# Four edits to a layernorm, windowed-attention and gated-FFN kernel: load order of the inputs, duplicated columns on GpSimd, a third early tile, and another rule for placing the value products

## The chip, the cores and the metric

The kernel runs on one core of a Trainium2 chip. A core has five engines that run their own instruction lists side by side and meet through semaphores: TensorE (PE in the profile; PEld are its weight loads), VectorE (DVE), ScalarE (ACT), GpSimd (POOL) and SyncE (SP, which here only issues DMAs). The metric is the device time of one execution in microseconds. Before the change three runs gave 557.07 (median), 558.04 and 556.71.

## The reference

The input x is 2048 rows of 576 bf16 values. It is normalised by row, and two branches read the result; x plus their product is the output.

```
xn = layernorm(x)                                   # eps 1e-5, no scale, no shift
qkv = xn @ wqkv                                     # 576 -> 3 x 32 heads x 18
s  = softmax(mask(q k^T / sqrt(18))) v @ wo         # key within the last 256 rows, not after the query
g  = silu((sigmoid(xn @ w_gate) * (xn @ w_up)) @ w_down)    # 576 -> 4608 -> 576
out = x + s * g
```

## The kernel before

**Chunks.** The rows go in four chunks of 512 (c = 0 to 3), each of four blocks of 128. For each chunk there are: normalising and transposing x; the value projection ("v"); five groups of query and key projections ("qk"); scores, exponentials and masks for eight groups of four heads ("sc", "ex", "mk"), each group in five score bins; two *value-product runs* ("pv"), each for four head groups, 256 TensorE instructions in chunk 0 (8 key blocks) and 384 in the others (12); the output projection ("wo"); 36 gate-and-up tiles of 128 hidden columns ("f1", each in two halves, "f10" and "f11"); and the down projection ("f2"). Weights for gate and up are read from HBM again in each chunk, two tiles at a time (`weights`), w_down only once.

**Pairs.** Every product has a contraction of 576 = 64 + 4 x 128 rows. TensorE is used as two halves of 64 rows: `pair` (the matmul of line 124) sends a matmul to each half, and the two run together. For the odd 64 rows both halves need the same data, so x is kept with its first 64 columns twice: `xnr` has 640 columns, 0 to 63 a duplicate ("dup") of 64 to 127. The remainder weights (`wgr`) are the matching 64 rows.

**The opening (chunk 0).** `load_x` issues the four x blocks first, all with `X_PRIO` 0. For each block, `build_ln` computes statistics (VectorE, lines 537 to 543, then a power on POOL, line 545; block 2 instead in two passes on ScalarE with small steps on POOL, lines 596 to 600), normalises on VectorE (`norm`, line 553), copies the duplicate on VectorE (`f_dup`, line 557), transposes on TensorE (line 609) and evicts to `xnT` (line 586; ScalarE, the last block on VectorE). Meanwhile `warm` keeps TensorE busy with 43 pairs on zeros and 10 more behind the first transposes. `NEARLY` = 2 tiles are "early": cut into four parts of 128 rows, so each part can start when its block of xnT is there. Around the last part `ahead` puts the first half of the next tile.

**The order of the work.** Nothing here loops on the chip. `build_graph` makes all operations with their dependencies, a duration and a priority (10 ns for each step of it), and `schedule` places them in Python: among those ready on an engine it takes the one with the smallest start time plus priority, at planned times. Each engine's instruction list is then fixed, and on the chip each operation waits on semaphores for what it needs. So the planner's estimates set the order, not the durations. A DMA's planned landing is its issue, 2.5 us and its bytes, plus a `slack` of its own; the moves of attention outputs (`oT<-o2T`) have 1.0 us.

**PSUM.** It has four units of two banks. Pool S (units 0, 1) serves transposes, projections and scores, pool F (2, 3, 1) the tiles and the down projection, pool V (any two) the value products.

**Placing value-product runs.** TensorE's instructions are counted in `at`. `fits` looks at the marks 193 + 256 k of that count: a run may start only where at most `FETCH_MAX` = 248 of its instructions lie in the 320 before any mark. If it doesn't fit, other operations go first until it does.

## Time and profile before

| | |
|---|---|
| time, median of 3 (lowest, highest) | 557.07 us (556.71, 558.04) |
| the profiled execution | 556.95 us, span 555.7 us |
| TensorE busy | 550.3 us, 99% of the span |
| VectorE, ScalarE, GpSimd busy | 58%, 49%, 38% of the span |
| DMA | 75.87 MB, mean 137 GB/s; 228 to 272 GB/s in the first seven fortieths of the span |
| first transposes, first tile | 5.70 us, 7.50 us |
| last matmul group | ends at 553.21 us |

A line of the chain gives start, duration, and the engine, tile and line that held the chain there; "issue" is time in which nothing that the profile shows was waited for. A line of the timeline gives start, duration, engine, line, operation, output tile <- inputs, shape, count, and in brackets how long the engine was idle before and what ended that. A line of the stretches gives the stretch, its length, TensorE's busy time in it (matmuls that start in it), the granted clock as a share, the share of DMA time in use, and GB/s. Matmul ends are modelled, so waits are best read from their starts. Times in the texts that have no line beside them are from the trace's single records: starts of matmuls, packets of a DMA queue, and landings.

### The profile page before, as it was taken

To read this page: it belongs to the slowest core of one execution; us is meant where nothing else is said; L and a number is where in the kernel's file an instruction comes from. 1 tells how busy PE (TensorE), PEld (TensorE's weight loads), DVE (VectorE), ACT (ScalarE), POOL (GpSimd) and SP (SyncE) were. 2 spreads that over 40 slices of the span, in tenths; PEclk is the share of its full clock that TensorE was granted. 3 is DMA by queue.
4 is the path that set the end of the run, shared out by engine and by line. 5 is a ranking of instruction groups with operands and counts; after the bars stand their busy time and mean duration, and the time that the engine had idled before them with its cause. 6 is when DMAs were issued, how large, how long until landed. Compare 5 with 4: busy or idle time off the path is not lost.

```text
span 555.7 us, 19419 instructions
## 1 busy us (share of the span) xinstructions
PE 550.3 (99%) x8342; PEld 339.3 (61%) x8342; DVE 323.4 (58%) x782; ACT 272.4 (49%) x379; POOL 208.7 (38%) x360
## 2 busy tenths in 40 slices
PE   8999999999999999999999999999999999999998
PEld 7454445777555654467775554447788644454787
DVE  5467567745858667537645567557535865474011
ACT  4246564442646647553455646654555477423201
POOL 5634343845424336434531517540922280011000
DMA  8999999442267654671243646554132255532010
GB/s 228 252 272 239 258 241 246 126 95 40 53 169 232 176 160 133 189 129 34 51 134 106 197 125 184 155 151 106 41 97 61 75 156 151 164 86 77 2 45 24
DMA packets 141213, 75.87 MB, mean 137 GB/s; under 512 B 43676, under 2 KB 139260, under 8 KB 141128
## 3 DMA queue, kind: packets, MB, share of 16 engines
q1 hardware_dynamic: 133704, 68.71, 46.9%
q0 software_dynamic: 7424, 5.92, 4.1%
q8 instruction: 66, 1.08, 0.8%
q14 instruction: 19, 0.16, 0.1%
HBM read 63.18 MB, written 2.36 MB: 118 GB/s over the span
## 4 chain that ended last, share of the span: by engine, by line
PE 96%; DMA 1%; POOL 1%; DVE 1%; issue 0%; ACT 0%
PE ps L124 93%; PE ps L813 3%; DMA oT<-o2T 1%; DMA x<-in_A_x_dram 0%; POOL kx L727 0%; POOL qk L286 0%; POOL oT L286 0%; DVE small L537 0%; DVE small L539 0%; DVE xnr L553 0%; PE ps L609 0%; DVE xnr L557 0%; DVE small L541 0%; ACT thf L1083 0%; DVE small L543 0%
## 5 line engine op out<-in xcount | busy, mean ns | idle before, releaser
L124 PE MATMUL ps<-xnT,wgs 64*128 64x512 bf16 (+1 forms) x2400 | 283.8, 368 | 0.1
L763 ACT ACTIVATE expr<-ps 128x1024 bf16<-128x1024 f32 (+4 forms) x160 | 154.9, 968 | 79.2 <-PE ps L124 77.5
L124 PEld LDWEIGHTS ps<-xnT,wgs 64*128 64x128 bf16 x2400 | 113.3, 94 | 111.9 <-issue 0.8
L124 PE MATMUL ps<-wd_sb,hT 64*128 64x288 bf16 (+2 forms) x2448 | 154.0, 276 | 0.0
L970 ACT ACTIVATE tring<-ps 128x512 bf16<-128x512 f32 x144 | 86.1, 598 | 125.4 <-PE ps L124 122.6
L973 DVE SCALAR_TENSOR_TENSOR hT<-tring,ps 128x512 bf16<-128x512 bf16 x144 | 98.6, 685 | 78.1 <-ACT tring L970 75.5
L286 POOL DMA_DIRECT2D qk<-qd x160 | 82.8, 524 | 150.8 <-PE ps L124 145.4
L124 PEld LDWEIGHTS ps<-wd_sb,hT 64*128 64x128 bf16 x2448 | 113.1, 94 | 28.0
L776 DVE TENSOR_TENSOR expr<-expr,mask 128x128 bf16<-128x128 bf16 (+2 forms) x240 | 64.5, 295 | 68.7 <-ACT expr L763 67.7
L286 POOL DMA_DIRECT2D oT<-o2T x72 | 36.9, 519 | 106.2 <-DVE o2T L849 51.4
L727 POOL TENSOR_SCALAR kx<-kprev,small 128x256 bf16<-128x256 bf16 x64 | 60.5, 955 | 7.8 <-PE ps L124 6.8
L124 PE MATMUL ps<-qk,kx 64*128 64x320 bf16 (+1 forms) x704 | 59.2, 254 | 0.0
L124 PE MATMUL ps<-xnT,wgr 64*128 64x512 bf16 (+1 forms) x300 | 55.9, 367 | 0.0
L124 PEld LDWEIGHTS ps<-qk,kx 64*128 64x128 bf16 x704 | 31.8, 94 | 25.8 <-ACT expr L763 1.3
L124 PE MATMUL ps<-xnT,wqg 64*128 64x512 bf16 (+1 forms) x320 | 37.7, 355 | 0.0
L648 DVE CAST qd<-ps 128x1024 bf16<-128x1024 f32 (+1 forms) x20 | 22.3, 1116 | 7.2 <-PE ps L124 7.2
L727 DVE TENSOR_SCALAR kx<-qk,small 128x512 bf16<-128x512 bf16 x64 | 22.2, 370 | 6.1 <-PE ps L124 5.8
L124 PEld LDWEIGHTS ps<-xnT,wgr 64*128 64x128 bf16 x300 | 14.8, 94 | 16.6
L841 DVE STREAM_TRANSPOSE ot<-ps 128x512 f32<-128x512 f32 x32 | 20.1, 685 | 7.4 <-PE ps L813 7.4
L849 DVE STREAM_TRANSPOSE o2T<-o 128x512 bf16<-128x512 bf16 x32 | 22.7, 708 | 0.5
L124 PEld LDWEIGHTS ps<-xnT,wqg 64*128 64x128 bf16 x320 | 15.2, 94 | 12.0 <-issue 0.3
L1085 DVE TENSOR_TENSOR thf<-thf,s_attn 128x576 bf16<-128x576 bf16 (+2 forms) x5 | 2.0, 399 | 34.2 <-ACT thf L1083 34.2
(68 smaller groups left out, 294.7 us busy)
## 6 DMA issues: line engine op xcount, KB each, us to landing
wgs<-in_B_w_gate_dram SPq DMA_DIRECT2D x72, 256.0 KB, 3.5
wgs<-in_B_w_up_dram SPq DMA_DIRECT2D x72, 256.0 KB, 4.0
wd_sb<-in_B_w_down_dram SPq DMA_DIRECT2D x9, 576.0 KB, 5.8
wqg<-in_A_wqkv_dram SPq DMA_DIRECT2D x32, 128.0 KB, 3.2
qk<-qd POOLq DMA_DIRECT2D x100, 36.0 KB, 2.5
wgr<-in_B_w_gate_dram SPq DMA_DIRECT2D x36, 64.0 KB, 2.6
wgr<-in_B_w_up_dram SPq DMA_DIRECT2D x36, 64.0 KB, 3.0
wvo<-in_A_wqkv_dram SPq DMA_DIRECT2D x4, 576.0 KB, 4.9
```

The source lines that it names most:

```text
L124: res = eng.matmul(outs[i], lhs(ROWS[t], i), rhs(ROWS[t], i), start=start, stop=stop, tile_position=(64 * t, 0))
L286: o = self.op(eng, DMA_ISSUE_NS[eng], lambda e: e.dma_start(dst, src), name, deps, prio, nbytes=nbytes)
L648: return eng.tensor_copy(dst, self.both(h, n))
L727: return e.tensor_scalar(self.kx[:, sx, pos:pos + n_ // SW, t, :], src.rearrange("p (s k) -> p s k", k=SW), self.half[:, t:t + 1], None, A ...
L763: return eng.activation(self.expr[:, se, :, lo * SW:NT], self.both(h, NT)[:, :, lo * SW:NT], ACTF.Exp, scale=SM_SCALE)
L776: return eng.tensor_tensor(e_, e_, m_, ALU.mult)
L813: res = eng.matmul(outs[i][p0:p0 + VH, cols], self.v_aug[ROWS[i], o:o + VH], self.expr[ROWS[i], se, t, cols], start=m == 0, stop=m == len( ...
L841: return e.transpose(self.ot1[:, p1, :], self.halves(hp, NT, un)[i])
L849: t2 = op("DVE", dve_ns(NT), lambda e, p2=p2, p3=p3: e.transpose(self.o2T[:, p3, :], self.o2[:, p2, :]), f"ot2:{c}:{pr}:{i}", deps=[on, d3 ...
L970: th = op("ACT", act_ns(NT), lambda e: e.activation(self.tring[:, st, :], bank(h, 0), ACTF.Tanh, scale=0.5), f"th:{c}:{ft}", deps=[pg, dt_ ...
L973: mu = op("DVE", dve_ns(NT), lambda e: e.scalar_tensor_tensor(self.hT[:, ft, :], self.tring[:, st, :], 1.0, bank(h, 1), ALU.add, ALU.mult) ...
L1085: q2 = op("DVE", dve_ns(w, 2.0), lambda e: e.tensor_tensor(t, t, s_, ALU.mult), f"fq2:{nm}", deps=[th, self.op_s[sb]], prio=0)
```

## The change

What the planner's tables and rules change to:

- The fourth x block gets priority 1.8 and is thereby issued behind the first gate and up weights and the two remainders. In the opening, landings of x and of the first four weight loads are planned by one running total of bytes (256 bytes per ns) with a fixed latency each, and no longer by single slacks.
- In chunk 0 the duplicate is computed on POOL, from x and the statistics (`norm_rem`), and no longer copied from the normalised block; transposes wait for both.
- Three tiles are early. The third is cut in two parts: rows of blocks 0 to 2, and of block 3. The first half of the tile behind them takes PSUM unit 0 (pool_a). One warm-up pair less.
- `fits` asks for time: the instructions of each 320 before a mark must last at least 6.1 us by plan, or 4.25 us while less than 256 tile instructions of the chunk are left. Each instruction of a run counts 6.3 ns, one behind it 54 or 30.6 ns, those before it as planned.
- Moves of attention outputs are planned with 1.8 us of slack (before 1.0); the spacing of scores, some durations on VectorE and POOL, the release of PSUM units (100 ns for pools S and V, before 60) and the size of the remainder loads are planned with other numbers.

The core of the diff; what is left out are unused names and the plumbing of new fields:

```diff
-FETCH_MAX = 248
+FETCH_NS = (6100.0, 4250.0)
+RUN_NS = 6.3
+STEP_NS = (54.0, 30.6)
...
-X_PRIO = (0, 0, 0, 0)
+X_PRIO = (0, 0, 0, 1.8)
...
-DUP_ACT = ()
+DUP_POOL = (0, 1, 2, 3)
...
-NWARM = (43, 10)
-NEARLY = 2
-FIRST_SLACK_NS = (-800.0, -1500.0)
+NWARM = (42, 10)
+NEARLY = 3
+OPEN_NS = 2000.0
+OPEN_BYTES_PER_NS = 256.0
+X_LAT_NS = (300.0, 800.0, 800.0, 800.0)
+W_LAT_NS = 1000.0
...
-PARTS = (((0, 1), (1, 2), (2, 3), (3, 4)),) * NEARLY
+PARTS = (((0, 1), (1, 2), (2, 3), (3, 4)),) * 2 + (((0, 3), (3, 4)),)
...
-SPACE_NS = (2000, 2000, 2000, 1700)
+SPACE_NS = (1900, 1700, 2200, 1800)
...
+        self.late = PE_IN_NS if name == "F" else POOL_IN_NS
...
-                free.append((max(now, max(r.end for r in h.rel) + PE_IN_NS), self.units.index(u), u))
+                free.append((max(now, max(r.end for r in h.rel) + self.late), self.units.index(u), u))
...
         self.pool_f = Pool("F", [2, 3, 1], last)
+        self.pool_a = Pool("F", [0], last)
...
-        return [self.dma(dst[ROWS[1 - t], :], src[0:RD, :], RD * src.shape[1] * 3, name, lane + (t,), deps=deps, prio=prio)
+        return [self.dma(dst[ROWS[1 - t], :], src[0:RD, :], RD * src.shape[1] * 2, name, lane + (t,), deps=deps, prio=prio)
...
+            def norm_rem(e, mean=mean, rstd=rstd, x_in=x_in, sn=sn, op0=ALU.add if on_act else ALU.subtract):
+                return e.tensor_scalar(self.xnr[:, sn, 0:RD], x_in[:, 0:RD], mean, rstd, op0, ALU.mult)
...
-            dup_act = c == 0 and i in DUP_ACT
-            dup = op("ACT" if dup_act else "DVE", act_ns(RD) if dup_act else 180, f_dup, f"ln:dup:{st}", deps=[ap], prio=pr)
-            self.ln_dup = dup
+            if c == 0 and i in DUP_POOL:
+                dup = op("POOL", 300, norm_rem, f"ln:dup:{st}", deps=[rs, ag, dn], prio=pr)
+            else:
+                dup = op("DVE", 180, f_dup, f"ln:dup:{st}", deps=[ap], prio=pr)
+            self.ln_dup = [ap, dup]
...
-                o.slack = 1000.0
+                o.slack = 1800.0
...
-                   prio=3 if part is None else 1, odeps=chain[half] if part is None else list(behind), acq=acq,
+                   prio=3 if part is None else 1 + ft / 2, odeps=chain[half] if part is None else list(behind), acq=acq,
...
-                        ahead = self.pool_f.hold()
+                        ahead = self.pool_a.hold()
...
-    @staticmethod
-    def fits(at, n):
-        ahead = (FETCH_AT - at) % FETCH
-        parts = [ahead] if n >= ahead else []
-        edge = ahead
-        while edge < n:
-            parts.append(min(n, edge + FETCH) - max(0, edge - FETCH_AHEAD))
+    def fits(self, at, n, st, places, ffn):
+        def when(p):
+            if p < at:
+                return next(t0 + (p - a0) * w for a0, t0, w in reversed(places) if a0 <= p)
+            return st + TURN_NS + min(p - at, n) * RUN_NS + max(p - at - n, 0) * STEP_NS[ffn]
+        edge = at + (FETCH_AT - at) % FETCH
+        while edge - FETCH - FETCH_AHEAD < at + n:
+            if edge > at and when(edge) - when(edge - FETCH - FETCH_AHEAD) < FETCH_NS[ffn]:
+                return False
             edge += FETCH
-        return max(parts, default=0) <= FETCH_MAX
+        return True
...
-                    if o.run and not self.fits(at + len(self.new_waits(o, known)) // 2, o.run):
+                    st = max(free[e], ready_t[o.cidx])
+                    if o.run and not self.fits(at + len(self.new_waits(o, known)) // 2, o.run, st, places, int(ffn[phase] < FETCH)):
...
+                if o.lat is not None:
+                    moved = max(moved, stt + o.est + 700.0) + o.nbytes / OPEN_BYTES_PER_NS
+                    o.end = moved + o.lat
```

## The prediction

> **What bounds the kernel now.** I read the page first (who is busy), then stretches of the span (where TensorE is not), then the chain and TensorE's timeline in those places. The profiled execution took 556.95 us for a span of 555.70, so 1.25 us lie outside the span; it stands 0.12 us under the median of 557.07.
>
> ```profile
> PE 550.3 (99%) x8342; PEld 339.3 (61%) x8342; DVE 323.4 (58%) x782; ACT 272.4 (49%) x379; POOL 208.7 (38%) x360
> ...
> q8 instruction: 66, 1.08, 0.8%
> ...
> PE 96%; DMA 1%; POOL 1%; DVE 1%; issue 0%; ACT 0%
> ```
>
> TensorE is the bound, and no other engine is near. The second line (packets, MB, share) matters for the placing rule: 66 packets of 16 KB, one for each 256 of TensorE's 16,950 instructions, are its own instruction fetches.
>
> ```profile
> core 0: us, PE busy (x), PEclk, DMA share, GB/s
> 6.00:12.10 6.10, 5.27 (x188) 1.00 0.93 259
> 12.10:100.00 87.90, 87.90 (x1038) 1.00 1.00 252
> 100.00:200.00 100.00, 99.44 (x1418) 1.00 0.48 127
> 200.00:553.00 353.00, 352.89 (x5620) 1.00 0.40 108
> ```
>
> After 12.1 us TensorE is idle for 0 + 0.56 + 0.11 us out of 541. Starts of matmuls show a little more, as a wait under a running matmul isn't idle here: 0.73 us at 160.20, 0.23 at 496.51, 0.20 at 423.58, and six of 0.03 to 0.09; about 1.3 us. That and the opening are all that a change can win while the matmuls stay the same.
>
> ```profile
> 7.10 0.19 DVE xnr L557
> ...
> 7.34 0.32 PE ps L609 x10
> ...
> 9.95 0.22 PE ps L609 x10
> 10.28 0.06 issue
> 10.34 3.70 PE ps L124 x82
> ...
> 154.49 5.16 DMA oT<-o2T
> 159.65 0.56 issue
> 160.20 4.84 PE ps L124 x61
> ```
>
> This is the chain. The copy of the duplicated columns ends the wait before the second transposes. At 10.28 TensorE waits for nothing that is shown: the starts jump from 10.06 to 10.34 at its instruction 449. In the packet records the first fetch runs from 7.64 to 8.85, and instruction 129, 320 before, started at 4.33: the fetch is asked for 320 instructions ahead, started 3.3 us later, and the instructions could run 6.0 us after. At 160.20 the output projection waits for moved attention outputs.
>
> ```profile
> 5.70 0.32 PE L609 MATMUL ps<-ident,xnr 64*128 64x64 bf16 x10 [0.28 <-DVE xnr L557]
> 7.34 0.32 PE L609 MATMUL ps<-ident,xnr 64*128 64x64 bf16 x10 [0.76 <-DVE xnr L557]
> 7.50 0.95 PE L124 MATMUL ps<-xnT,wgs 64*128 64x128 bf16 x24
> 8.32 0.33 PE L609 MATMUL ps<-ident,xnr 64*128 64x64 bf16 x10
> 9.85 0.32 PE L609 MATMUL ps<-ident,xnr 64*128 64x64 bf16 x10
> 13.23 1.03 PE L124 MATMUL ps<-xnT,wgs 64*128 64x512 bf16 x8
> ```
>
> Useful work runs from 7.34. Up to 13.24 there are 144 matmuls 128 wide (72 pairs at 0.056), three transposes of a block (0.155 each) and the first half of tile 2 (4 pairs at 0.216): 5.36 us of work in 5.89, so 0.53 lost, of which 0.23 is the fetch and 0.10, at 8.05, the remainder weights, which landed at 7.75.
>
> **The change, part by part.**
>
> *Load order.* The fourth x block's issue (0.47 us on SP) goes behind the two first weights and their two remainders. These four move up 0.47 us, and 147 KB (0.57 us at the stretch's 259 GB/s) leave their way: they landed at 6.14, 7.13, 7.30, 7.75 and should by some 0.5 us earlier. The wait at 8.05 goes (0.10). The fourth block, landed at 5.01, comes at about 7.5 to 8; behind it stand 2.5 us of statistics and normalising (rows of 0.45, 0.44, 0.20, 0.15, 0.57, 0.43), a transpose and an eviction of 0.49, so its columns are ready near 11.4. The second weights stay fifth and sixth: they landed at 9.76 and 10.61, and I keep that. POOL's memsets follow that block and end some 0.5 us later than 15.9; their first users start after 18.
>
> *Duplicated columns on GpSimd.* Four copies (0.18 to 0.20) leave VectorE; four 128x64 tensor_scalars join POOL. None is in the trace: 0.20 to 0.25 (128x1) and 0.24 (an affine select of 128x64) lie below, 0.955 (128x256) above. I take 0.35, by the near rows. They run beside the normalising (0.43), but not freely:
>
> ```profile
> L727 DVE TENSOR_SCALAR kx<-qk,small x64: 342/349/597, 33.2 to 459.8; 128x512 bf16<-128x512 bf16 x64
> ```
>
> This row's instruction, of the same kind as the normalising, takes 0.35 us alone and up to 0.60 where POOL's own kx runs beside it: 0 to 0.25 us of penalty. A block's path gains between 0.20 and -0.05; I take +0.1. Behind POOL's first new one waits the mean for ScalarE's second pass (5.43), 0 to 0.1 late.
>
> The Trainium skill's "SBUF — State Buffer", section "SBUF: two separate sides", says the two engines' shared port pair is an exclusive lock and the loser blocks wholly. By it the new instruction would follow the normalising: the first transposes at about 5.9 instead of 5.70, the second at about 7.4, no gain. The rows here show overlap with stretching (0.60 us inside POOL's 0.94), not one behind the other, so the row decides.
>
> *When useful work starts.* The first tile needs block 0's eviction, which ScalarE began at 6.49 and ended at 7.17, behind its statistics (5.71 to 6.58). An earlier transpose doesn't move that. But the second transposes then stand at about 7.0, not in front of the tiles at 7.34: tiles start at 7.25 (bounds 6.9, if the eviction goes first, and 7.55).
>
> *Three early tiles.* Tile 2 costs 9 pairs of 384 columns (0.163 each, 1.46 us) and 9 of 128 (0.50) instead of 9 of 0.216 (1.94): +0.02. From 7.25: 4.03 + 2 transposes 0.31 + 1.46 + 0.50 + 0.86 (tile 3's first half) = 14.42. Before, the same content stood at 13.24 + 1.94 = 15.18. Without any wait the opening gains 0.76. But instruction 449 holds: with 4 fewer warm-up instructions and the last transposes behind it, 88 tile matmuls (2.46) and one transpose (0.155) come before it, so TensorE is there at 9.87 and waits for the fetch until 10.34: 0.47 us. Twenty matmuls later, at 10.90, it wants the second weights (landed 10.61; the remainders' wait ended 0.30 after landing, so 10.9): no more wait. Net -0.29 us. Bounds: -0.76 with no wait, +0.3 with weights 0.6 later.
>
> *Output moves' allowance, 1.0 to 1.8 us.* The plan puts the output projection 0.8 later behind tiles that are ready; the 0.73 wait at 160.20 is covered if the move takes again 5.16 us. Ends 0 and -0.73; I take -0.55, since every later step is placed anew.
>
> *Value-product runs.* Eight runs (1.79 us for 128 matmuls, 2.40 for 192; one took 2.49) keep their matmuls. Before, at most 248 of a run's instructions lay in a fetch's 320; now 320 must last 6.1 us, or 4.25 when tiles are nearly used up. With 54 ns per other instruction that is about 240, slightly narrower. From fetch request to edge the narrowest windows took 3.59, 3.96, 4.26, 4.55, 5.24 and 5.80 us, with the packet 1.46 to 1.84 us ahead of the edge; only the 5.80 one shows a loss (2.49 for 2.40). So there is 0.1 us to win; some runs move by 256 instructions (7.8 to 13.8 us), which tiles and the down projection cover while there are any. The rest (spacing of scores, VectorE's and POOL's estimates) only reorders: the 0.6 us of small waits is redrawn, 0 +/- 0.6.
>
> The Trainium skill's "Runtime: NRT & Kernel Launch", section "Instruction fetch mechanics", has crossing a 256-instruction block mostly hidden; by it the 0.47 above would not exist and the opening would gain 0.76. The jump at instruction 449 is in the trace, so I keep the wait.
>
> Sum: -0.29 - 0.55 - 0.1 + 0.0 = -0.94; 556.95 - 0.94 = 556.0 in the profiled run's terms, 556.1 beside the median; rounded up for waits that a new order brings, **556.2 us**.
>
> **Rivals.**
> 1. *All waits go.* Tiles from 6.9, instructions and second weights in time: -0.76 - 0.35; -0.73 and -0.5 of the rest: -2.2, 554.9 us. For it: all these waits depend on arrivals, and the request stands 320 instructions ahead. Against: 93% of the DMA time is used in 6.0 to 12.1, so a fetch isn't likely quicker.
> 2. *It doesn't do what it says.* The lock or the late second weights eat the opening (0 to +0.3), and the projection waits again for its moves: 557.0 to 557.6 us. For it: the moves are slow where loads of 250 GB/s run, and 1.0 to 1.8 was one allowance for all chunks.
> 3. *Slower: a value-product run refused at a narrow slot.* In chunk 1 the second run (253.05, a window of 3.59 us, under 4.25) must move by 256 instructions at 0.0306, 7.8 us. Its output projection, at 276, moves to 284, and the chunk's down projection ends at 289. One refusal fits in; from the second on (15.6 against 13) TensorE has 2.6 us or more without work, if the next chunk's tiles aren't ready: 556.2 + 2.6 = 558.8, up to 564 for a whole slot. Against: the next chunk's tiles start at 288 with their inputs long there, and in the last chunk 24 us lie between the last run (488) and the projection (512).
>
> **How the numbers follow.** Forecast as summed (555.4 to 557.0): 0.54. Rival 2: 0.20. Rival 1: 0.11. Rival 3: 0.15. The range, 555.0 to 558.3, leaves out about half of rival 1 and nearly all of rival 3. A difference of 0.3% (1.67 us) is about what a measurement of this kernel can tell from no change: faster means under 555.4, rival 1 alone, 0.11; slower over 558.74, rival 3, 0.15; the same, 0.74.
>
> **What the profile would show.** Right: first tile at 7.2 to 7.3, a jump of 0.3 to 0.5 us near instruction 449 at about 10.3, tile 2 at 10.9, no wait over 0.3 us for oT, all runs at 1.79 and 2.40. Wrong: VectorE's normalising at 0.55 or more with the second transposes after 7.4; a wait of TensorE on the second weights; a run longer than 2.5 us; TensorE idle by over 1 us in any stretch after 13.

## The result and the profile after

The changed kernel takes 558.09 us (median of 22 executions, 557.38 to 558.92); the kernel before, in 22 executions beside it, 557.33 us (556.71 to 558.04). The ratio is 1.0015, 95% interval 1.0009 to 1.0021. So the change costs 0.76 us. That is less than the 0.3% that the prediction took for what can be told from no change, but the interval excludes the forecast gain, and the sign is the other one. Below, each time has in brackets its number of executions, its ratio to the kernel before in executions beside it (medians of 557.25 to 557.82 us) and the ratio's 95% interval. What is read from a trace is one execution.

The profiled execution took 558.21 us for a span of 556.96 us, 1.26 us longer than the span of before. That is more than the medians differ by: this execution stands 0.12 us above its median, and the one of before 0.38 us below. The page of the changed kernel, the lines shown of before (busy time of the engines; packets, MB and share of TensorE's own instruction fetches; the chain by engine):

```profile
PE 551.1 (99%) x8358; PEld 347.3 (62%) x8358; DVE 322.7 (58%) x778; ACT 271.9 (49%) x379; POOL 212.7 (38%) x364
...
q8 instruction: 66, 1.08, 0.8%
...
PE 96%; DMA 2%; POOL 1%; DVE 0%; issue 0%; ACT 0%; POOLq 0%
```

Four copies left VectorE and four instructions joined GpSimd, as the diff says. There are still 66 fetches. DMA is now 2% of the chain. The same stretches as before (length, TensorE busy, granted clock, DMA share, GB/s):

```profile
core 0: us, PE busy (x), PEclk, DMA share, GB/s
6.00:12.10 6.10, 5.02 (x170) 1.00 0.93 257
12.10:100.00 87.90, 87.76 (x1061) 1.00 0.96 239
100.00:200.00 100.00, 99.78 (x1428) 1.00 0.54 139
200.00:553.00 353.00, 352.43 (x5557) 1.00 0.39 108
```

Up to 12.1 us TensorE is busy for 0.25 us less than before, from 100 to 200 us for 0.34 us more, and elsewhere a little less. The chain of waits names the places:

```profile
5.11 0.74 POOL xnr L565
...
8.37 0.56 POOL xnr L565
8.93 0.14 issue
9.07 0.32 PE ps L623 x10
...
97.16 6.27 DMA wd_sb<-in_B_w_down_dram
103.42 0.14 issue
...
251.46 1.52 PE ps L827 x104
252.98 0.42 issue
253.40 1.03 PE ps L827 x65
```

Three things are new: GpSimd's duplicates (L565) stand in the opening's chain, where VectorE's copy had stood; a piece of w_down ends a wait at 103.4; and a value-product run is interrupted at 253 while TensorE waits for nothing that the profile shows. The wait for moved attention outputs at 160.20 is gone. The opening on TensorE's timeline (transposes are L623, tiles L130):

```profile
5.99 0.32 PE L623 MATMUL ps<-ident,xnr 64*128 64x64 bf16 x10 [0.28 <-POOL xnr L565]
...
7.61 0.32 PE L623 MATMUL ps<-ident,xnr 64*128 64x64 bf16 x10 [0.74 <-POOL xnr L565]
7.76 0.95 PE L130 MATMUL ps<-xnT,wgs 64*128 64x128 bf16 x24
...
9.07 0.32 PE L623 MATMUL ps<-ident,xnr 64*128 64x64 bf16 x10 [0.30 <-POOL xnr L565]
...
11.52 0.32 PE L623 MATMUL ps<-ident,xnr 64*128 64x64 bf16 x10
...
15.78 0.59 PE L130 MATMUL ps<-xnT,wgs 64*128 64x512 bf16 x3
```

Before, the four transposes started at 5.70, 7.34, 8.32 and 9.85, and the first tile at 7.50. The content that ends at 15.78 now (three tiles and the first half of tile 3) ended at 15.18 in the count of the prediction: 0.60 us lost, where 0.76 was to win without waits.

To see where the rest went I use one sum for all kernels. *Lost time* up to t is t minus the time that the matmuls started by then need at full rate: N/2.4 + 2.7 ns for a pair with N columns, which is what undisturbed pairs take in these traces, and 1.79 or 2.40 us for a value-product run. Transposes count as work too, the warm-up counts as lost, so only differences mean something (us):

| up to | 17 | 95 | 110 | 200 | 270 | 340 | 430 | 553 |
|---|---|---|---|---|---|---|---|---|
| before | 7.64 | 7.67 | 7.69 | 8.49 | 8.66 | 8.73 | 9.13 | 9.40 |
| after | 8.23 | 8.50 | 9.17 | 9.23 | 10.00 | 10.17 | 10.27 | 10.67 |
| after minus before | +0.59 | +0.83 | +1.48 | +0.74 | +1.34 | +1.44 | +1.14 | +1.27 |

The last figure is the difference of the spans. Its steps, from the starts of matmuls: the opening +0.59; two waits of 0.23 us at 86.81 and 97.59 and one of 0.39 us for w_down at 103.56, with smaller ones +0.89; the 0.73 us at 160.20 no longer lost, -0.74; the run at 251.4, 2.98 us long for 2.40, +0.60; the run at 322.2 (2.57), +0.10; two small losses of before (0.20 at 423.58, 0.09 in a run) gone, -0.30; a wait of 0.29 us at 461.10 for one of 0.23 at 496.51, +0.13.

### The profile page after: what moved, and what is told of

The parts are those of the page before. It is cut to its first block, busy times and chain, and to the rows that moved or that the text cites. A ratio compares the mean times of both kernels' runs of the same rounds, so it can differ in the third digit from the quotient of the medians.

```text
span 557.0 us, 19453 instructions
## 1 busy us (share of the span) xinstructions
PE 551.1 (99%) x8358; PEld 347.3 (62%) x8358; DVE 322.7 (58%) x778; ACT 271.9 (49%) x379; POOL 212.7 (38%) x364
## 4 chain that ended last, share of the span: by engine, by line
PE 96%; DMA 2%; POOL 1%; DVE 0%; issue 0%; ACT 0%; POOLq 0%
PE ps L130 93%; PE ps L827 3%; DMA wd_sb<-in_B_w_down_dram 1%; DMA x<-in_A_x_dram 0%; POOL xnr L565 0%; POOL small L554 0%; PE ps L623 0%; ACT tring L984 0%; DVE hT L987 0%; POOL small L614 0%; DVE small L546 0%; DVE kx L741 0%; DVE small L548 0%; ACT thf L1097 0%; DVE thf L1099 0%
## 5 line engine op out<-in xcount | busy, mean ns | idle before, releaser
L130 PE MATMUL ps<-xnT,wgs 64*128 64x512 bf16 (+1 forms) x2416 | 283.7, 366 | 0.3
L130 PEld LDWEIGHTS ps<-xnT,wgs 64*128 64x128 bf16 x2416 | 117.0, 94 | 107.6 <-PE ps L130 1.1
L130 PE MATMUL ps<-wd_sb,hT 64*128 64x288 bf16 (+2 forms) x2448 | 153.9, 276 | 0.2 <-DMA wd_sb<-in_B_w_down_dram 0.2
L130 PEld LDWEIGHTS ps<-wd_sb,hT 64*128 64x128 bf16 x2448 | 115.1, 94 | 27.0 <-issue 0.4
L130 PE MATMUL ps<-qk,kx 64*128 64x320 bf16 (+1 forms) x704 | 59.6, 254 | 0.0
L130 PE MATMUL ps<-xnT,wgr 64*128 64x512 bf16 (+1 forms) x302 | 56.5, 366 | 0.0
L130 PEld LDWEIGHTS ps<-qk,kx 64*128 64x128 bf16 x704 | 32.5, 94 | 25.4 <-ACT expr L777 0.3
L130 PE MATMUL ps<-xnT,wqg 64*128 64x512 bf16 (+1 forms) x320 | 37.8, 355 | 0.0
L130 PEld LDWEIGHTS ps<-xnT,wgr 64*128 64x128 bf16 x302 | 15.4, 94 | 16.1
L130 PEld LDWEIGHTS ps<-xnT,wqg 64*128 64x128 bf16 x320 | 15.8, 94 | 11.7 <-issue 0.6
L130 PE MATMUL ps<-wvo,oT 64*128 64x288 bf16 x256 | 19.9, 283 | 0.0
```

The lines of the kernel that those rows point to most:

```text
L130: res = eng.matmul(outs[i], lhs(ROWS[t], i), rhs(ROWS[t], i), start=start, stop=stop, tile_position=(64 * t, 0))
```

## Theories

*Theory after the first profile.* The loss has three independent sources. (1) GpSimd's instruction is longer than the copy that it replaces and delays block 0, ScalarE's pass and block 2. (2) Fetches of TensorE's instructions come too late in value-product runs, and the new order puts them worse. (3) The new order has waits of its own in chunk 0. *Rivals*: the load order costs the opening; the new placing rule alone makes the runs long; loads beside the fetches make them late; the runs are long for want of scores.

To follow instruction fetches I counted TensorE's instructions as the kernel does. *Mark k* is instruction 449 + 256 k, the first one of a fetched packet. A packet's time minus the time of the instruction 320 ahead of the mark is called its lag here, though that request isn't a record of its own.

## Experiments on the opening

**The duplicates back on VectorE, planned anew.** `DUP_POOL = (0, 1, 2, 3)` becomes `()`.

> The changed kernel with the duplicated columns copied on VectorE again. Theory P (GpSimd's new instruction, 0.74 us where 0.30 was planned, and the small steps that queue behind it are what the opening lost): first transposes back from 5.99 to about 5.7, first tile from 7.76 to about 7.5, third transposes from 9.07 to about 8.4, and the end of the opening (start of tile 3's second half) from 15.78 to 14.9-15.2, so 0.6 to 0.9 us faster than the changed kernel, about 557.3. Theory O (load order or the third early tile cost the opening): the first tile and 15.78 move by less than 0.2. The value-product runs keep their long ones, 0.3 to 0.8 us in all, in both.

561.20 us (6 executions, 1.0067, 1.0049 to 1.0085). Transposes at 5.64, 7.27, 8.24 and 10.89, first tile at 7.42; lost time at 17 us 7.46, that is 0.77 less than in the changed kernel, which is GpSimd's part, and 0.18 less than before. Of the 0.18, 0.10 is a shorter wait at mark 0 (0.12 us at 10.31, before 0.22 at 10.34) and 0.08 the earlier first tile (7.42 for 7.50), so the load order and the third early tile show no gain of their own. The time is 4 us above the 557.3 expected: the planner made another order of everything behind, and this one lost 1.46 us at mark 8 (92.94) and 2.47 us in two runs (458.6: 3.94 us; 514.6: 3.31). The price of an edit can't be read from the total here when the order is planned anew. Where it is said below, the order is held.

**GpSimd's duplicates alone, in the kernel before.** `norm_rem` on POOL added to before.py, nothing else. The order is planned anew, but all eight runs start within 1.7 us of where they did.

> The kernel before with only the duplicated columns moved to GpSimd. Theory P: the instruction takes 0.55 to 0.75 us beside VectorE's normalising; first transposes at 5.9-6.0 instead of 5.70, the end of the opening (13.24 before, start of tile 2's second half) later by 0.3 to 0.7 us; the time 557.6 to 558.0. Theory O: the end of the opening within 0.2 us of 13.24.

559.94 us (5 executions, 1.0035, 1.0022 to 1.0048). Transposes at 5.94, 7.59, 9.05, 10.40, GpSimd's instructions 0.73, 0.78, 0.55 and 0.74 us, 1.27 us more lost at 17 us than before (0.3 to 0.7 were expected), of which 0.35 and 0.71 are waits of the transposes at 9.05 and 10.40. The profiled execution is the fastest of the five. The cost of the opening in the changed kernel is GpSimd's, then, with the old load order and two early tiles too.

**GpSimd's instruction behind the normalising, not beside it.**

```diff
-                dup = op("POOL", 300, norm_rem, f"ln:dup:{st}", deps=[rs, ag, dn], prio=pr)
+                dup = op("POOL", 300, norm_rem, f"ln:dup:{st}", deps=[rs, ag, dn, ap], prio=pr)
```

> The changed kernel with GpSimd's instruction made to wait for VectorE's normalising of the same block, so that the two no longer start together. Theory L (a shared port is held by VectorE's instruction and GpSimd stands still for it): it takes 0.35 to 0.40 us now and ends at the same time as before, near 5.9. Theory S (the instruction itself needs 0.74 us on GpSimd): it takes 0.7 us again and ends at about 6.2, and the opening is 0.3 us longer.

One execution. GpSimd's timeline in the changed kernel, beside the normalising:

```profile
4.42 0.57 POOL L554 TENSOR_TENSOR small<-small 128x1 f32<-128x1 f32 x1 [2.60 <-DVE small L552]
5.11 0.74 POOL L565 TENSOR_SCALAR xnr<-x,small 128x64 bf16<-128x64 bf16 x1
5.83 0.24 POOL L611 TENSOR_SCALAR small<-small 128x1 f32<-128x1 f32 x1
...
7.71 0.56 POOL L614 TENSOR_TENSOR small<-small 128x1 f32<-128x1 f32 x1
8.37 0.55 POOL L565 TENSOR_SCALAR xnr<-x,small 128x64 bf16<-128x64 bf16 x1
```

and in this kernel, alone:

```profile
5.68 0.60 POOL L565 TENSOR_SCALAR xnr<-x,small 128x64 bf16<-128x64 bf16 x1
...
10.67 0.59 POOL L565 TENSOR_SCALAR xnr<-x,small 128x64 bf16<-128x64 bf16 x1 [0.63 <-POOL small L554]
```

and all four of this kernel (shortest, median and longest in ns):

```profile
L565 POOL TENSOR_SCALAR xnr<-x,small x4: 398/597/632, 5.7 to 10.7; 128x64 bf16<-128x64 bf16 x4
```

So alone the instruction takes 0.59 and 0.60 us (blocks 3 and 0), and in the changed kernel, beside VectorE's normalising, 0.74 in blocks 0, 1 and 3: 0.35 was too little by 0.25 even without any contention. Block 2's, which adds its mean where the others subtract it, took 0.40 us here, behind the normalising, and 0.55 beside it in the changed kernel. So VectorE's instruction, begun 0.06 to 0.08 us ahead, costs GpSimd's some 0.15 us in either form. The 0.24 us step for ScalarE (L611), at 5.43 before, stands at 5.83; ScalarE's second pass at 6.10 instead of 5.71; the product behind it (L614) at 7.71 instead of 6.95, and with it block 2. VectorE's instruction of the same time isn't stretched in the changed kernel:

```profile
5.03 0.43 DVE L562 TENSOR_SCALAR xnr<-x,small 128x576 bf16<-128x576 bf16 x1
```

The time of this execution (563.45 us) says nothing on the opening: 3.93 us of it lie in runs.

**The order held, duplicates copied by VectorE.** The changed kernel is planned as it is; only then the four instructions are exchanged.

```diff
         self.prog = prog
+        for ap, dup, copy in self.swap:
+            prog["POOL"].remove(dup)
+            prog["DVE"].insert(prog["DVE"].index(ap) + 1, dup)
+            dup.eng, dup.fn, dup.deps = "DVE", copy, [ap]
```

> The changed kernel with every engine's order held as it is, except that the four duplicates are copies on VectorE right behind their normalising. Theory P (GpSimd's instruction and its queue cost the opening, the rest of the loss is elsewhere): the opening loses 0.7 to 0.8 us less than in the changed kernel (lost time at 17 us 7.4-7.5 instead of 8.23), and as the order behind it is the same, the time falls by the same or a little less, to 557.3-557.6. Theory D (the loads hold chunk 0, so an earlier start only waits later): lost time at 110 us stays near 9.2 and the time within 0.2 of 558.1.

558.82 us (12 executions, 1.0026, 1.0016 to 1.0036). Transposes at 5.71, 7.36, 8.35 and 11.21, first tile at 7.53, but lost time at 17 us 8.02, only 0.21 better: what GpSimd no longer took, mark 0 took, with a start that waits for nothing shown:

```profile
9.86 0.60 PE L130 MATMUL ps<-xnT,wgs 64*128 64x128 bf16 x15
10.91 0.45 PE L130 MATMUL ps<-xnT,wgs 64*128 64x128 bf16 x9 [0.45 <-issue]
```

Behind it the runs lost 2.74 us in the profile (0.82 in the changed kernel), although the order is the same. Why is the question of the last section of experiments.

**The fourth x block ahead again, in that kernel.** Its load is moved back behind the third.

> The run before this one but one (order held, duplicates on VectorE) with the fourth x block loaded behind the third again, still with three early tiles. If the load order alone is worth what it was costed at (0.1 us of the wait for the remainder weights, and nothing for tile 2), the opening's lost time is 0.1 to 0.3 us larger than in that run, through the first gate and up weights 0.4 to 0.6 us later; if it is worth nothing, within 0.05.

558.75 us (8 executions, 1.0032, 1.0020 to 1.0043). TensorE waited 0.31 us at 8.30 for the remainder weights (0.11 at 8.08 with the new load order), so the new load order saves 0.2 us against this kernel. Against the kernel before, which has 0.10 us at this place with the old load order, it saves nothing there. Yet lost time at 17 us is 8.02 in both: mark 0 came at 10.92 in both, and what is won ahead of it is waited for at it.

**The first fetch asked for earlier, in the kernel before.** The 43 warm-up pairs of 128 columns become 32 of 64 and 11 of 256, which takes the same time but has TensorE at instruction 129 at 2.76 instead of 4.33 us.

> The kernel before, order and count of instructions held, but the 43 warm-up pairs are 32 of 64 columns and then 11 of 256 instead of 43 of 128, so that TensorE passes instruction 129 at about 2.9 us instead of 4.33. Theory W (the first fetch is asked for when instruction 129 goes, and its arrival is a wall for instruction 449): the wall moves forward by 1.2 to 1.4 us, the jump at instruction 449 (0.23 us in the profile before, 0.6 to 1.05 in others of the same opening) is gone, the lost time at 17 us is 7.3-7.4 instead of 7.64, and the time falls by 0.3 to 1.0 us under 557.3. Theory V (the first fetch comes when the memory system lets it, near 10.3 to 11.2): the jump stays and the time within 0.2 of 557.3.

557.24 us (12 executions, 0.9998, 0.9990 to 1.0007). At mark 0 only 0.07 us is left of the jump; on TensorE's timeline the 24 matmuls around it run through:

```profile
9.80 0.32 PE L609 MATMUL ps<-ident,xnr 64*128 64x64 bf16 x10
9.95 0.98 PE L124 MATMUL ps<-xnT,wgs 64*128 64x128 bf16 x24
10.77 0.22 PE L124 MATMUL ps<-xnT,wgr 64*128 64x128 bf16 x2
```

Lost time at 17 us fell from 7.64 to 7.44, 0.15 of it at mark 0. But the wall didn't move by the 1.2 to 1.4 us of theory W: instruction 449 ran at 10.14, before at 10.34. The packet's record starts at 7.68 and ends at 8.83, before at 7.64 and 8.85, although instruction 129 ran 1.6 us earlier. In the four kernels with this warm-up the packet starts at 7.63 to 7.95, in the eleven with instruction 129 at 4.3 at 7.55 to 9.06. So TensorE waited for its instructions, as the prediction read it; that asking earlier brings them earlier isn't shown. By 553 us nothing of the gain is left (9.39 against 9.40), and the median moved by less than the executions scatter.

**The same in the held kernel with VectorE's copies.**

> The changed kernel with its order held, duplicates on VectorE, and the same warm-up as in the run before this one (31 pairs of 64 columns, 11 of 256). Theory W: the jump of 0.62 us at instruction 449 goes, the opening's lost time falls from 8.02 to 7.3-7.5, which is what the load order and the third early tile are worth without GpSimd; the time falls by 0.3 to 0.8 us under the 558.8 of the held order. Theory V: no change in either.

559.02 us (11 executions, 557.66 to 561.92; 1.0034, 1.0019 to 1.0049). The wait at mark 0 is down to 0.05 us here: lost time at 17 us is 7.63, against 8.02 with it and 8.23 in the changed kernel. So all opening edits together, without GpSimd's instructions and nearly without that wait, are 0.60 us better than the changed kernel, but no better than the kernel before (7.64) and 0.19 worse than it with the same warm-up (7.44): the last block's transposes, whose x now comes later, are waited for at 10.92, for 0.19 us. The total didn't follow. The profile can't say why, as it is of the fastest of the eleven executions; in it 1.0 us was lost in the runs at 455.4 and 511.8.

## Experiments on the value-product runs

**The new placing rule alone, in the kernel before.** `fits`, `FETCH_NS`, `RUN_NS` and `STEP_NS` of the changed kernel, nothing else.

> The kernel before with only the new placing rule (6.1 us, or 4.25 near the end of a chunk's tiles). Theory F (the new rule lets runs in whose fetch comes late): the sum that runs take over 1.79 and 2.40 rises from 0.10 us to 0.4 or more, time 557.7 to 558.3. Theory T (late fetches hit any placing by the traffic of the moment): the sum lies anywhere from 0.1 to 1 on other runs than in the changed kernel. No effect at all: within 0.2 of 557.3.

559.43 us (7 executions, 1.0031, 1.0019 to 1.0042). All eight runs start later, by 2 to 17 us, and two of them lost 0.67 and 0.85 us, each in the middle:

```profile
216.32 1.56 PE L815 MATMUL ps<-expr,v_aug 64*19 64x320 bf16 x116
218.40 1.06 PE L815 MATMUL ps<-expr,v_aug 64*19 64x64 bf16 x76 [0.52 <-issue]
...
501.44 1.75 PE L815 MATMUL ps<-expr,v_aug 64*19 64x320 bf16 x135
503.80 0.95 PE L815 MATMUL ps<-expr,v_aug 64*19 64x192 bf16 x57 [0.61 <-issue]
```

Another 0.68 us went at mark 8, behind the first run (94.55). The opening, the same as before, lost 1.05 us at mark 0 in this execution (11.20).

**The old rule in the changed kernel.**

> The changed kernel with the placing rule of before (at most 248 instructions in a fetch's 320). Theory F (the rule of 4.25 us lets a run in whose fetch comes too late): the sum that the runs take over 1.79 and 2.40 falls from 0.82 us to under 0.2, the time to about 557.4. Theory T (fetches come late with the DMA traffic of the moment, whatever the rule): the sum stays at 0.3 or more, on other runs, and the time within 0.3 us of 558.1. The opening stays at 15.78 in both.

558.24 us (12 executions, 1.0017, 1.0000 to 1.0033): as the changed kernel. Its runs stand where the changed kernel's stand up to shifts by earlier waits (327.1 and 256.3 us at 3.03 and 2.99), so the rule did not place the changed kernel's runs; the new order did. This profiled execution, at 563.48 us the longest of its 12, waited 3.47 us for w_down, of which more below.

**Less traffic beside the runs.** The loads of gate and up weights in chunks 1 to 3 read 16 of 128 partitions.

> The changed kernel with the same order of instructions, but the gate and up weight loads of chunks 1 to 3 cut to 16 of 128 partitions, so that tiles there multiply what chunk 0 left behind; output is not the reference's. Theory T (a fetch of TensorE's instructions comes late because it queues behind other transfers): from chunk 1 on the delay from the request to the fetch packet falls from 1.2-4.3 us to 1.0-1.5 everywhere, the three long value-product runs of 2.98, 2.57 and 2.47 us come to 2.40, and the time falls by 0.7 to 1.0 us. Theory R (the delay belongs to the placing or to TensorE): the same runs stay long.

557.88 us (10 executions, 1.0006, 0.9997 to 1.0015). The other runs lost 0.09 us together, the last one (511.8) 0.96. At the mark in the run at 251 the lag fell from 2.4 to 1.4 us, and the run took 2.40, as theory T has it. But between 505 and 516 us, around the last run, the only DMA traffic is two fetches, as in the changed kernel (packets of that stretch, and their queue):

```profile
DMA packets 2, 0.03 MB, mean 3 GB/s; under 512 B 0, under 2 KB 0, under 8 KB 0
## 3 DMA queue, kind: packets, MB, share of 16 engines
q8 instruction: 2, 0.03, 1.0%
```

and the one that the run waited for lagged 3.0 us, more than twice the 1.3 of the changed kernel at the same mark. From 150 us on the mean lag is 2.1 us here and 2.3 in the changed kernel. So other loads may add to a lag, but a lag of 3.0 us needs none; theory T doesn't account for the long runs.

**All marks 48 instructions earlier in the work.** The last 12 of 42 warm-up pairs are split into 24 of half the width; the order is held.

> The changed kernel with its order of work held; the last 12 of the 42 warm-up pairs are split into 24 pairs of half the width, so 48 more instructions stand ahead of all useful work and every 256th instruction, at which a new piece of TensorE's list must be there, falls 48 instructions earlier in the work. The computation is the same and the warm-up takes the same time (12 x 0.107 = 24 x 0.054 us). Theory (late fetches make the long value-product runs): taking the changed kernel's own times between instructions, the windows of 320 around the runs shrink by up to 48 x (54 - 6.3) ns = 2.3 us on one side of a run and grow on the other; set against the lags of 1.3 to 3.7 us (tenth to ninetieth percentile of the runs so far) and 2.5 us from a packet's start to use, the sum over all runs rises by about 3.8 us against unshifted marks. That sum comes out too high for the unshifted kernel (5.7 where 0.8 was measured), so I expect 2 to 5 us more in the runs, 560 to 563 us in all, with the first of each pair of windows as the one that is short. Rival (the long runs come from something that goes with the order: scores not ready, loads beside them, the rows' cost itself): the runs stay as they are in the changed kernel, 0.6 to 1.4 us over 1.79 and 2.40 in all, and the time stays at 558 us. In the opening the instruction that was the 449th is the 497th and the wall stands 24 matmuls earlier in the work: 0 to 0.7 us more there on either theory.

560.35 us (4 executions, 1.0042, 1.0025 to 1.0059). Neither side's numbers: the runs lost 0.12 us, not 0.8 and not 2 to 5. The losses moved with the marks, out of the runs and behind them: 0.54 us at 208.17, 0.35 at 330.32 and 0.18 at 394.85, 1.19 us with the runs.

```profile
207.19 0.60 PE L130 MATMUL ps<-xnT,wgs 64*128 64x512 bf16 x3
208.17 0.81 PE L130 MATMUL ps<-xnT,wgs 64*128 64x512 bf16 x5 [0.38 <-issue]
```

This one stands 3 us behind the end of its run, in tiles, with no semaphore to wait for. In the traces of all sixteen kernels there are 35 jumps of over 0.2 us in TensorE's starts after 7.7 us without a semaphore wait, and all 35 stand at a mark, within one instruction of it. That settles what makes a run long by more than 0.2 us: late instructions, neither scores nor the rows themselves. The sizes were not what I had worked out from lags drawn at random; why is seen below. Of the 2.8 us by which this profiled execution is longer than the changed kernel's, 1.66 are again in the wait at the down projection (2.05 us at 105.58 for 0.39) and 0.45 in the opening.

## Experiments on w_down and on four instructions

The last of the nine pieces of w_down is issued at 97.16 us in the changed kernel, 92.33 before, because the tile that releases it comes later in the new order. It landed at 98.10 before. In kernels with the changed kernel's order it landed at 101.69, 102.57, 103.23, 103.42, 105.44 and 106.53, with the small loads at 99.34, and TensorE wants it at about 103.2. The chain of the old-rule kernel above:

```profile
99.11 7.42 DMA wd_sb<-in_B_w_down_dram
106.53 0.14 issue
106.66 4.41 PE ps L131 x41
```

**The last piece earlier, in the changed kernel.** It is issued behind the two weight loads at 89.6 us, ahead of four moves and five loads.

```diff
+        last, prior = self.op_wd[-1], self.op_wd[-2]
+        prog["SP"].remove(last)
+        prog["SP"].insert(prog["SP"].index(prior) + 3, last)
+        last.deps = list(prior.deps)
```

> The changed kernel with one DMA moved: the last of w_down's nine pieces is issued ahead of four moves of attention outputs and five loads (near 90.2 instead of 97.16 us) and no longer waits for a later tile's product. Theory (the new order makes that piece late): it lands before 100, TensorE's wait on wd_sb (0.39 at 103.56 in the changed kernel's profile, 2.05 and 3.47 in two other executions of the same order) goes, and the median falls from 558.1 by 0.3 to 0.8, to 557.3 to 557.8 us. Rival (nothing follows from the piece: the loads it is moved ahead of, gate and up weights, the x rows and the moves, become late instead): a wait of 0.3 us or more on one of those, or on oT at 160, takes its place, and the median stays at 558.0 to 558.6 us.

558.55 us (11 executions, 1.0013, 1.0004 to 1.0021). The piece lands at 97.21, the wait is gone, nothing took its place, and the profiled execution has a span of 556.4, 0.54 less than the changed kernel's, as lost time has it (10.13 for 10.67). But it is the fastest of the eleven, and the ratio can't be told from the changed kernel's 1.0015. The wait is real in single executions; for the median nothing is shown.

**The same in the held kernel with VectorE's copies and the early fetch.**

> The same move of w_down's last piece in the held version with the duplicates copied on VectorE and the early first fetch, which took 559.02 us (557.66 to 561.92) although its opening is 0.66 us better than the changed kernel's. If the late piece makes its high executions: a median of 557.2 to 558.0 us and none above 559.5. If the instruction fetches at its value-product runs make them (0.5 us each at 457 and 513 in its profile, with lags that differ from execution to execution): the median stays at 558.5 to 559.2 with executions above 560.

558.73 us (11 executions, 557.70 to 559.36; 1.0016, 1.0007 to 1.0025). The high executions went (561.92 before this edit), which the first theory had; the median didn't come under 558, which the second had. In the profile the opening is at 7.66, w_down causes no wait, and five marks in runs lose 2.80 us.

**Four instructions put back.** Without GpSimd's part TensorE has less to wait for in front of the transposes, and its list is shorter there: by the records 16,981 instructions where the changed kernel has 16,984, so every mark falls three instructions later in the work. One more warm-up pair of 64 columns (16,985) undoes that but for one instruction.

> The held version with copies on VectorE, early first fetch and early last piece of w_down, with one warm-up pair of 64 columns more: four more instructions, so that the marks stand at the same matmuls as in the changed kernel. Theory (four instructions decide, since the windows at the runs stand at 6.0 to 6.2 us, just where the fetch comes): losses at marks in the runs fall from 2.80 to about 0.8 in a profile as in the changed kernel, and the median, with an opening 0.66 and w_down 0.4 better than the changed kernel's, comes to 557.0 to 557.6 us. Rival (the shift is worth 4 x 0.048 = 0.19 us at a mark at most, and the lags differ for other reasons): 1.5 us or more in the runs and a median of 558.3 to 559.0 us.

557.36 us (11 executions, 556.56 to 557.98; 1.0001, 0.9992 to 1.0010). With four instructions of warm-up more, of themselves 0.06 us that nothing waits for, the kernel is faster by 0.15% or 0.8 us going by the ratios (the medians differ by 1.4, but the kernel before was 0.4 us faster beside the second, too; the intervals just overlap), and by 1.6 us in the profiled executions. The run at 457 on TensorE's timeline, without them

```profile
457.00 1.58 PE L830 MATMUL ps<-expr,v_aug 64*19 64x320 bf16 x118
459.22 1.05 PE L830 MATMUL ps<-expr,v_aug 64*19 64x64 bf16 x74 [0.64 <-issue]
```

and with them

```profile
456.53 2.47 PE L832 MATMUL ps<-expr,v_aug 64*19 64x320 bf16 x192
```

The run at 250 still loses 1.19 us in this execution, and it alone. One profile of each doesn't fix the size: the held kernel with the early fetch has its marks where the first of the two has them and lost only 1.0 us in its runs. Lost time of this section's kernels (us):

| up to | 17 | 95 | 110 | 200 | 270 | 340 | 430 | 553 |
|---|---|---|---|---|---|---|---|---|
| changed, piece early | 8.24 | 8.42 | 8.69 | 8.75 | 9.65 | 9.70 | 9.73 | 10.13 |
| copies, early fetch, piece early | 7.66 | 8.06 | 8.32 | 8.51 | 9.42 | 10.14 | 10.17 | 11.67 |
| the same, four instructions back | 7.65 | 7.92 | 8.19 | 8.39 | 9.66 | 9.66 | 9.69 | 10.10 |

The first and the last of these have the same order, the same early piece and, but for one instruction, the same marks; they differ in the duplicates and the first fetch. Lost time at 17 us differs by 0.59 us, and the ratios, 1.0013 and 1.0001, by 0.12% or 0.67 us (their intervals just overlap, 1.0004 to 1.0010). In the profiles the gap has shrunk to 0.03 by the end, mostly in the run at 250. So the opening is large enough to explain nearly all of what the change costs in the medians; that it does is likely and not shown beyond the intervals. The last kernel is as fast as the kernel before, no faster; none of the versions beats both.

## Why the prediction was wrong, step by step

| term | forecast, us | profile, us |
|---|---|---|
| opening | -0.29 (-0.76 to +0.3) | +0.59 |
| output moves | -0.55 (-0.73 to 0) | -0.73 |
| value-product runs | -0.1 | +0.72 |
| rest, redrawn | 0 +/- 0.6 | +0.69 (what is left) |
| sum | -0.94 | +1.27 |

Two steps failed. GpSimd's instruction, taken at 0.35 us, took 0.74 beside the normalising and delayed what stood behind it on its queue, so the opening lost 0.59 us instead of winning 0.29. The value-product runs, taken to have only 0.1 us to win, lost 0.72 us more, to late instructions.

*Load order: right in the landings, not in their worth.* The four early weight loads landed at 5.55, 6.60, 6.81 and 7.09, between 0.49 and 0.66 us earlier for "some 0.5"; x's last block landed at 7.69, within the 7.5 to 8; the second weights landed at 10.61 as kept. But the wait of 0.10 us at 8.05, which was to go, stands at 8.31 with 0.08: it wasn't for the remainder weights. Where TensorE does wait for them, with the fourth block loaded ahead again, it goes on 0.09 us after they land (8.21 and 8.30), not 0.30.

*Duplicated columns on GpSimd: the step that turned the opening's sign.* "I take 0.35, by the near rows." It measured 0.59 to 0.60 alone and 0.74 beside the normalising in three blocks, 0.40 and 0.55 in the fourth. The bounds, 0.20 and 0.955, held it; the choice between them didn't. The near rows were of other operations or of one column: an instruction of the same kind with a per-row operand and 256 columns took 0.955, and the new one with 64 columns, as it ran, is nearer to that than to 0.24. "A block's path gains +0.1" became a loss of 0.29 (transposes at 5.99 for 5.70). "The mean for ScalarE 0 to 0.1 late" became 0.40 (5.83 for 5.43), for the instruction stands ahead of it on GpSimd's queue; from that came ScalarE's eviction of block 0, at 6.87 for 6.49, and the first tile at 7.76, where 7.25 with an upper bound of 7.55 was forecast. The third new instruction and the late ScalarE pass put block 2's transposes at 9.07, a wait of 0.46 us.

The exclusive lock of the Trainium skill's "SBUF — State Buffer", section "SBUF: two separate sides", which the prediction weighed, gave transposes at "about 5.9". The page has the lock against VectorE instructions in a two-port mode or with two inputs in SBUF; which mode the normalising ran in no run here shows. The transposes came at 5.99, but not by that way. In the changed kernel VectorE normalises from 5.03 to 5.46; a GpSimd instruction that began its 0.59 us behind that would have ended at 6.05, and it ended at 5.85. Plainest is the kernel with the instruction behind its own block's normalising: there block 1's ran from 7.69 to 8.32 (0.63 us) and VectorE's normalising of block 2 from 7.72 to 8.23 (0.51 for 0.43), so neither stood still for the other. Overlap with stretching was right; the instruction's own length was not. The row that had shown it, VectorE's kx (mean 0.37 us before), reads nearly the same after:

```profile
L741 DVE TENSOR_SCALAR kx<-qk,small 128x512 bf16<-128x512 bf16 x64 | 21.4, 364 | 10.7 <-PE ps L130 10.5
```

*Three early tiles: no gain shown.* Without any wait the sum put the start of tile 3's second half at 14.42. With VectorE's copies and nearly no wait at mark 0 (the held kernel with the early fetch) it stands at 15.19, and the same content stood at 15.18 before: the tiles begin at 7.56, not 7.25, 0.32 us go in waits at 8.11, 10.38 and 10.92, and the last 0.14 I can't place.

*When useful work starts: the wall is real, its place is not fixed.* The wait for instruction 449 was forecast at 0.47 us "until 10.34". In the changed kernel's profile it doesn't show, as GpSimd's delay brings TensorE there after the packet. Where that delay is taken away it shows at 10.91 and 10.92, in the new rule's kernel at 11.20; the packet starts 3.2 to 4.7 us after instruction 129 at 4.3, and 4.9 to 5.2 us after it where that instruction ran at 2.7. So a wait for instructions was right, against the "mostly hidden" of the Trainium skill's "Runtime: NRT & Kernel Launch", section "Instruction fetch mechanics" (of some 1,000 crossings in the sixteen traces 35 lose over 0.2 us), and the term "until 10.34" was one draw of a wide spread taken for a fixed time. The opening without GpSimd's part then gains 0.18 us (7.46 for 7.64, planned anew), gains nothing (7.63, order held, early warm-up) or loses 0.38 (8.02, order held, with the wall).

*Output moves: right in size, not for the forecast's reason.* The whole 0.73 went, the term's lower end. But the sum counted on a move of 5.16 us again, covered by a later projection. In the changed kernel the last move took 1.98 us and landed at 150.71, 3.80 us ahead of the projection. In the kernel before with the new placing rule alone, whose allowance is still 1.0 us, it took 1.97 and nothing waited either. What the allowance itself is worth no run shows.

*Value-product runs: wrong in sign.* "There is 0.1 us to win" took for granted that the runs could only get better from a state where the narrowest windows showed no loss. The windows and lags were in the working (3.59 to 5.80 us, packets 1.5 us ahead of the edge), and they say the opposite: nothing is in hand at these marks, so any new order can lose at them. The changed kernel lost 0.82 us in runs in its profile; other kernels with its order 0.77 to 2.80, and 0.12 with the marks 48 instructions earlier. In the changed kernel the rule, in nanoseconds or in instructions, isn't what decides: with the old one its runs stand where they stood and its time is the same. In the kernel before the new rule alone moved all eight runs and made it 0.31% slower.

*The rest, "redrawn, 0 +/- 0.6": above its range.* It came to +0.69. An order whose small waits are down to 0.6 us looks like a low draw: by 553 us the kernel before had lost 9.4 us, and four other kernels planned anew here 11.4 to 15.9, openings included. w_down's last piece is the instance: a tile that comes 4.8 us later makes a load late that had landed 5 us earlier.

*The rivals.* The second came nearest in time (557.0 to 557.6, measured 558.09) and half in kind: the opening was eaten, by GpSimd's instruction and its queue, neither by a lock nor by late weights, and the output projection didn't wait again. The first's terms add up to -2.34, not -2.2, and so to 554.7 us. The third, a run refused, didn't occur: the runs stand where the old rule has them, too. Slower through late instructions inside the runs wasn't on the list, though its place and its prices were.

## What to carry to other kernels

Price a moved instruction by the row of the same operation on the same engine, however much larger, before any small row of another operation, and follow its queue: here 0.2 to 0.4 us too little on GpSimd moved four more things. In an unrolled kernel bound by one engine, an edit that changes the number of instructions ahead of dense stretches moves every later fetch boundary; before a time is put down to the edit itself, hold the order and put the count back. A tuned order may be a low draw of its small waits, and a change that has everything planned again should be charged for the loss of that luck.

## What the runs showed of the hardware

TensorE's instruction fetches. The losses stand at the first instruction of each 256, and in the 35 cases that one ran 1.24 to 1.59 us after its packet's record ended. The lag from 320 instructions ahead to the packet's start ran from about 1 to 8 us. It is not a matter of chance at one place: at mark 52, in the run at 457, in the changed kernel's order it was 4.24 to 4.76 us in four held kernels, whose marks fall three instructions later, and 2.33 to 2.87 in four with the marks within one instruction of the changed kernel's place (1.31 in the one with smaller loads). At mark 58 the same kernels have 2.06 to 2.16 and 1.31 to 1.87 (2.98). What sets the lag stays open: it was 3.0 us with no other DMA in flight, and no experiment here told apart the other candidates, such as what TensorE runs when the request falls due.

GpSimd's 128x64 tensor_scalar with two per-row operands took 0.59 to 0.60 us alone where it subtracts and multiplies, and 0.40 (one instruction) where it adds and multiplies; its 128x256 one with one such operand took 0.955.

After the 3.47 us wait for w_down in the old-rule kernel TensorE's granted clock fell to about half for 3 us (stretches: length, busy time, granted clock, DMA share, GB/s):

```profile
100.00:106.60 6.60, 3.35 (x58) 1.00 0.94 275
106.60:108.00 1.40, 1.34 (x17) 0.74 0.41 110
108.00:111.00 3.00, 3.00 (x30) 0.55 0.57 164
111.00:115.00 4.00, 4.00 (x56) 1.00 0.39 90
```

so that this one late load cost that execution some 5 us (563.48 against its median of 558.24). The wait of 2.05 us in the kernel with the marks moved left the clock at 1.00. The Trainium skill's "TensorE: Matmul & The Clock Gate", section "Part 1: The HAM clock gate (the "warmup" mystery)", has the clock fall to half after an idle window of about 3.4 us; the 3.47 us here agree with it.
